# A decode block on Trainium2: the first weight load in two pieces, and exps that write the probability block themselves

## The chip, the cores and the metric

The kernel runs on one core of one Trainium2 chip. The metric is the device time of one execution, in microseconds. A core has five engines that run side by side, each with its own instruction queue: TensorE (PE, matmuls; PEld is its weight load), VectorE (DVE), ScalarE (ACT), GpSimd (POOL) and SyncE (SP), which here only issues transfers. Sixteen DMA engines move the data between device memory (HBM) and the core's memory of 128 partitions (SBUF). Engines wait for each other through semaphores.

## What is computed

One token passes through a transformer block: layer norm, attention over a cache of 4096 positions with 32 heads of 128, a residual, a second layer norm, a gated feed-forward part, a residual. All inputs are bf16.

```python
q = (layernorm(x) @ wq).reshape(B, Sq, Hq, Dh).transpose(0, 2, 1, 3)
scores = einsum("bhqd,bhkd->bhqk", q, k) * (Dh ** -0.5)
p = softmax(scores)
o = einsum("bhqk,bhkd->bhqd", p, v)
h = x + o.reshape(B, Sq, Hq * Dh) @ wo
h2 = h + (gelu(layernorm(h) @ w_gate) * (layernorm(h) @ w_up)) @ w_down
```

With a single token every weight and every cache entry is used once: 84 MB are read from HBM. The caches alone are 2 x 32 heads x 4096 x 128 x 2 bytes = 67 MB.

## The kernel before

**How the work is laid out.** The 32 heads are cut into eight groups of four. In a group, partition 32j + p holds head j's positions 128p to 128p + 127, so a group's K or V is a tile of 128 partitions of 32,768 bytes each (4 MB). Three slots hold such tiles in turn (`NSLOT`, L22). The order of loads is K0, V0, K1, K2, V1, K3, V2 and so on to K7, V6, V7 (L173 to L176): K runs one group ahead of V.

**The loads.** All large loads are issued by SP, in program order, on one queue. First comes wq (L172), 5 MB into `arena`, 128 partitions of 40,960 bytes. `issue` (L186) then issues cache loads as slots come free: load n waits for `consumed[n - 3]`, the last reader of the tile that lay in its slot. For a K tile that reader is the last product of the group on DVE, for a V tile the last matmul of `pv_group`. While SP waits for one slot, every later load waits behind it. The output projection's weights follow into `arena` (L387), and then the feed-forward weights into the slots. `emit({"sync": 2})` (L474) places SP's first two issues, wq and K0, ahead of the start barrier that all engines pass; SP's others come after it.

**The start.** `x_row` is loaded from ACT's queue; the layer norm runs on PE, DVE and ACT; `q_proj` (L260) waits for it and for wq, and leaves q in `qb`, one head's q repeated over its 32 partitions.

**A stage.** A group has four stages of 32 positions per partition. In stage s, `score_mult` (L274) multiplies K by q on DVE into `prod` (128x4096) and PE folds the 128 products of each position to 16 by eight matmuls with an identity matrix, into one of two PSUM banks. `score_exp` (L291) then sums the 16 on DVE into `sc` (L293). The program has stage s + 1's product ahead of stage s's sum on DVE.

**The end of a group.** After the fourth stage ACT takes one exp over the group's whole 128x128 scores into `pt` (L297) and adds up each partition's exps into a column of `RS`. DVE then multiplies `pt` by `own` (`block_diag`, L300): `own[p, j]` is 1 where partition p belongs to head j, otherwise 0. The result `p_bd` (128 x 128 x 4) holds, for each position, four columns, of which a partition fills only its own head's. `pv_group` (L306) uses it as the weights of 32 matmuls with V as the moving operand, on PE after the next group's folds; ACT copies the sums to SBUF (L319), and four small matmuls add them up (`head_sum`, L321). `own` comes from a select on POOL (L225) and a reduction on DVE (L233).

**Each half of the heads.** `sum_half` (L332) multiplies `RS` by `own`, sums it over the partitions by a matmul and takes the reciprocal; `finish_half` (L339) scales. Then come the output projection (L350), the second layer norm, the gated part and the down projection.

`P.op` records every instruction with the events that it waits for; `emit` writes them out engine by engine in the order of the program, so SP's issues all stand at L51 in the profile.

Of the kernel before, what the change touches and what calls it, by code (L numbers as in the profile page):

```python
# [5 lines left out]
FP32 = mybir.dt.float32  # L6
BF16 = mybir.dt.bfloat16
ALU = mybir.AluOpType
ACTF = mybir.ActivationFunctionType
AX = mybir.AxisListType  # L10

D = 640
H = 32
# [4 lines left out]
INV_SQRT_DH = 1.0 / math.sqrt(DH)  # L18
GELU_C0 = math.sqrt(2.0 / math.pi)
GELU_C1 = 0.044715  # L20
NG = 8
# [80 lines left out]
def bass_sequential_preLN__gqa_block_cached__glu_gated_geglu__decode_kernel(nc, A_x, A_k_cache, A_v_cache, A_wq, A_wo, B_x, B_w_gate, B_w_up, B_w_down, out):  # L102
    sb = lambda name, shape, dt: nc.alloc_sbuf_tensor(name, shape, dt)
    SLOT = 10 * DF
    slots = [sb("slot%d" % i, [128, SLOT], BF16) for i in range(NSLOT)]
    arena = sb("arena", [128, 5 * 4096], BF16)
    prod = sb("prod", [128, 4, 32, DH], BF16)
    qb = sb("qb", [128, NG, DH], BF16)
    sc = sb("sc", [128, 2, 128], FP32)
    pt = sb("pt", [128, 2, 128], BF16)  # L110
    own_t = sb("own_t", [128, 4, 32], BF16)
    own = sb("own", [128, 4], BF16)
    p_bd = sb("p_bd", [128, 2, 128, 4], BF16)
    RS = sb("RS", [128, NG], FP32)
    RT = sb("RT", [128, NG, 4], FP32)
    x_row = sb("x_row", [1, D], BF16)
    out_row = sb("out_row", [1, D], BF16)
    xx = sb("xx", [128, 10], FP32)
# [23 lines left out]
    ones_f = sb("ones_f", [128, 128], FP32)  # L142
    mean_f = sb("mean_f", [128, 128], FP32)
    ones_b = sb("ones_b", [128, 1024], BF16)
# [3 lines left out]
    zero_t = sb("zero_t", [128, 1], FP32)  # L148
    bank = [nc.alloc_psum_tensor("bank%d" % i, [128, 512], FP32) for i in range(8)]
    ps_f = [bank[0], bank[1]]  # L150
# [6 lines left out]
    ps_z = bank[6]  # L157
# [5 lines left out]
    P = Prog(nc)  # L163
    V = lambda fn, *d: P.op("vector", fn, *d)
    A = lambda fn, *d: P.op("scalar", fn, *d)
    T = lambda fn, *d: P.op("tensor", fn, *d)
    GP = lambda fn, *d: P.op("gpsimd", fn, *d)
# [1 line left out]

    A(lambda e: e.preload_act_table_set("natural_log_exp_and_others"))  # L170
    d_x = P.dma("scalar", x_row[:, :], A_x[0, :, :])
    d_wq = [P.dma("sync", arena[:, :], A_wq[:, :].rearrange("(p c) n -> p (c n)", c=5))]  # L172
    order = [("K", 0), ("V", 0), ("K", 1)]  # L173
    for G in range(1, NG - 1):
        order += [("K", G + 1), ("V", G)]
# [2 lines left out]
    landed, consumed = {}, {}  # L178
# [7 lines left out]
    def issue(upto):  # L186
        while state["next"] < min(upto, len(order)):
# [8 lines left out]
                         for i in range(parts)]  # L196
# [9 lines left out]
    c_eps = V(lambda e: e.memset(zero_t[:, :], 0.0))  # L206
    c_onesb = GP(lambda e: e.memset(ones_b[:, :], 1.0))
    c_idb = GP(lambda e: e.affine_select(id_b[:, :], ones_b[:, 0:128], pattern=[[1, 128]], compare_op=ALU.is_equal,
                                         fill=0.0, base=0, channel_multiplier=-1), c_onesb)
    c_idf = GP(lambda e: e.affine_select(id_f[:, :], ones_f[:, :], pattern=[[1, 128]], compare_op=ALU.is_equal,  # L210
                                         fill=0.0, base=0, channel_multiplier=-1), c_ones)
    c_sel = GP(lambda e: e.affine_select(sel[:, :, :], ones_b[0:16, :].rearrange("p (a b) -> p a b", a=8),
                                         pattern=[[-1, 8], [1, 128]], compare_op=ALU.is_equal,
                                         fill=0.0, base=0, channel_multiplier=-8), c_onesb)
    GP(lambda e: e.memset(hs[:, :, :], 0.0))
    c_hs = GP(lambda e: e.affine_select(hs_t[:, :, :], ones_f[:, 0:64].rearrange("p (a b) -> p a b", a=4),
                                        pattern=[[-32, 4], [-1, 16]], compare_op=ALU.is_equal,
                                        fill=0.0, base=0, channel_multiplier=1), c_ones)
    c_sel2 = GP(lambda e: e.affine_select(sel2[:, :, :], ones_b[0:64, 0:128].rearrange("p (a b) -> p a b", a=64),
                                          pattern=[[1, 64], [0, 2]], compare_op=ALU.is_equal,  # L220
                                          fill=0.0, base=0, channel_multiplier=-1), c_onesb)
    c_par = GP(lambda e: e.affine_select(par_t[:, :, :], ones_b[:, 0:128].rearrange("p (a b) -> p a b", a=2),
                                         pattern=[[-1, 2], [-2, 64]], compare_op=ALU.is_equal,
                                         fill=0.0, base=0, channel_multiplier=1), c_onesb)
    c_own = GP(lambda e: e.affine_select(own_t[:, :, :], ones_b[:, 0:128].rearrange("p (a b) -> p a b", a=4),  # L225
                                         pattern=[[-32, 4], [-1, 32]], compare_op=ALU.is_equal,
                                         fill=0.0, base=0, channel_multiplier=1), c_onesb)

    c_po = [V(lambda e, b=b: e.memset(bank[b][:, :], 0.0)) for b in (2, 4)]
    c_hs = V(lambda e: e.reduce_sum(hs[:, :, 12:16], hs_t[:, :, :].rearrange("p t (g j) -> p g j t", g=4), axis=AX.X), c_hs)  # L230

    V(lambda e: e.reduce_sum(par[:, :], par_t[:, :, :], axis=AX.X), c_par)
    V(lambda e: e.tensor_reduce(own[:, :], own_t[:, :, :], axis=AX.X, op=ALU.max), c_own)  # L233


    def x_cols(e):
# [32 lines left out]
    qc = A(lambda e: e.copy(qb[:, 4:8, :].rearrange("p g d -> p (g d)"), ps_q[1][:, :]), qd)  # L269


    folds, reds, exps, blocks, pvs, evs, hds = {}, {}, {}, {}, {}, {}, {}

    def score_mult(s):  # L274
        G, n = s // 4, pos[("K", s // 4)]
        kt = view(n)
        u = s % 4
        m = V(lambda e: e.tensor_tensor(  # L278
            out=prod[:, s % 4, :, :], in0=kt[:, 32 * u:32 * u + 32, :],
            in1=qb[:, G, :].unsqueeze(1).to_broadcast([128, 32, DH]), op=ALU.mult),  # L280
            landed[n][0], qa, qc, folds.get(s - 4))
        consumed[n] = m

        def fold(e):
            for b in range(8):
                i = e.matmul(ps_f[s % 2][:, :], id_b[:, :], prod[:, s % 4, :, 16 * b:16 * b + 16],  # L286
                             start=(b == 0), stop=(b == 7))
            return i
        folds[s] = T(fold, m, c_idb, reds.get(s - 2))

    def score_exp(s):  # L291
        G = s // 4
        reds[s] = V(lambda e: e.reduce_sum(  # L293
            sc[:, G % 2, 32 * (s % 4):32 * (s % 4) + 32], ps_f[s % 2][:, :].rearrange("p (g d) -> p g d", d=16), axis=AX.X),
            folds[s], exps.get(G - 2))
        if s % 4 == 3:
            exps[G] = A(lambda e: e.activation(pt[:, G % 2, :], sc[:, G % 2, :], ACTF.Exp, bias=zero_t[:, 0:1],  # L297
                                               scale=INV_SQRT_DH, accum_out=RS[:, G:G + 1]), reds[s], blocks.get(G - 2), c_eps)

    def block_diag(G):  # L300
        blocks[G] = V(lambda e: e.tensor_tensor(  # L301
            out=p_bd[:, G % 2, :, :], in0=pt[:, G % 2, :].unsqueeze(2).to_broadcast([128, 128, 4]),
            in1=own[:, :].unsqueeze(1).to_broadcast([128, 128, 4]), op=ALU.mult), exps[G], pvs.get(G - 2))


    def pv_group(G):  # L306
        n = pos[("V", G)]
        vt = view(n)
        po = ps_o[G % 2]
        parts = len(landed[n])  # L310
        for k in range(parts):
            def pv(e, k=k):
                for b in range(32 // parts * k, 32 // parts * (k + 1)):
                    a = 32 * (b % 4)
                    i = e.matmul(po[a:a + 16, :], p_bd[:, G % 2, 4 * b:4 * b + 4, :].rearrange("p g j -> p (g j)"),  # L315
                                 vt[:, 4 * b:4 * b + 4, :], start=(b < 4), stop=(b >= 28))
                return i
            pvs[G] = consumed[n] = T(pv, blocks[G], landed[n][k], evs.get(G - 2), *c_po)
        evs[G] = A(lambda e: e.copy(po_sb[:, G % 2, :], po[:, :]), pvs[G], hds.get(G - 2))  # L319

        def head_sum(e):  # L321
            g = G % 4
            for r in range(4):
                i = e.matmul(ps_a[0:16, 128 * (G // 4):128 * (G // 4) + 128], hs[:, r, 12 - 4 * g:28 - 4 * g],  # L324
                             po_sb[:, G % 2, 128 * r:128 * r + 128], start=(g == 0 and r == 0), stop=(g == 3 and r == 3))
            return i
        return head_sum
# [2 lines left out]
    zs = {}  # L330

    def sum_half(t):  # L332
        gs = slice(4 * t, 4 * t + 4)
        r = V(lambda e: e.tensor_tensor(out=RT[:, gs, :], in0=RS[:, gs].unsqueeze(2).to_broadcast([128, 4, 4]),  # L334
                                        in1=own[:, :].unsqueeze(1).to_broadcast([128, 4, 4]), op=ALU.mult), exps[4 * t + 3])
        z = T(lambda e: e.matmul(ps_z[0:16, 0:1], RT[:, gs, :].rearrange("p g j -> p (g j)"), ones_f[:, 0:1], start=True, stop=True), r)  # L336
        zs[t] = V(lambda e: e.reciprocal(rz[:, t:t + 1], ps_z[0:16, 0:1]), z)

    def finish_half(t):  # L339
# [20 lines left out]
    def scores(G):  # L360
        for i in range(4):
            score_mult(4 * G + i)
            if i >= 1:
                score_exp(4 * G + i - 1)
        score_exp(4 * G + 3)
        block_diag(G)
        issue(pos[("K", G)] + 1 + NSLOT)

    heads = None
    for kind, G in order:  # L370
        if kind == "K":
            scores(G)
            continue
        if G in (3, NG - 1):
            sum_half(G // 4)
        if heads is not None:
            hds[G - 1] = T(heads, evs[G - 1], c_hs, qa, qc)
        if G == 4:
            a0 = finish_half(0)
        heads = pv_group(G)  # L380
        issue(pos[("V", G)] + 1 + NSLOT)
# [22 lines left out]
             for a, lo, hi in ((0, 0, 4), (1, 0, 4), (2, 0, 3), (2, 3, 4))]  # L404
# [10 lines left out]
                                     in1=hT[:, 0:5].unsqueeze(1).to_broadcast([128, 128, 5]), op=ALU.mult), h, c_idf)  # L415
# [33 lines left out]
    def down(ms, qs=range(4)):  # L449
        def fn(e):  # L450
            for m in ms:
                for q in qs:
# [6 lines left out]
                              start=True, stop=True), g9, c_sel2)  # L459
# [11 lines left out]
    d_out = P.dma("sync", out[0, :, :], out_row[:, :], *os)  # L471
    P.op("sync", None, d_out)

    P.emit({"sync": 2})  # L474


# [26 lines left out]
```

## Time and profile before

| | us |
|---|---|
| median of three runs (lowest, highest) | 205.05 (204.47, 205.85) |
| the profiled execution: its time | 205.85 |
| its span, first to last instruction | 204.5 |
| busy: PE, DVE, ACT, POOL | 119.8, 106.5, 12.6, 4.3 |
| products on DVE, L278, 32 of them | 72.4 (2.28 each) |
| sums on DVE, L293, 32 | 22.0 (0.69 each) |
| mask multiplies on DVE, L301, 8 | 5.5 (0.69 each) |
| exps on ACT, L297, 8 | 3.2 (0.40 each) |
| wq from its issue to its landing | 15.9 |

The profile covers one execution. A group of instructions is a line of the kernel, an engine, an operation and a tile, with the number of instructions, their busy time and the mean of one; behind it stands how long the engine was idle before them and what ended that. "Chain" is the work that ended last, followed back from the last instruction to whatever released each step. The slices cut the span into 40 equal parts; a digit is a busy share in tenths, with 9 for 90% and more. In tables by stretch, the last two numbers are the DMA share and GB/s, and the one before them is the clock that TensorE was granted. A DMA packet is one contiguous run that one DMA engine moves.

### The profile page before, as it was taken

The numbers are of one execution on the slowest core, as the hardware profiler recorded it, in microseconds if no ns is written. First come the engines' busy times: TensorE is split into PE (matmuls) and PEld (weight loads), VectorE is DVE, ScalarE is ACT, GpSimd is POOL, SyncE is SP. The second block draws the span as 40 slices with busy tenths as digits, with TensorE's granted clock in tenths as the row PEclk, the third lists the DMA queues.
The fourth block names the chain that finished last, engine by engine and source line by source line (L and its number), as shares of the span: only waits on it lengthen the run. The fifth ranks groups of instructions, "written<-read, shape, count | busy, mean of one in ns | idle before, by whom it ended". The sixth has DMA issues, their size and how long they took to land.

```text
span 204.5 us, 2243 instructions
## 1 busy us (share of the span) xinstructions
PE 119.8 (59%) x1010; PEld 58.7 (29%) x1010; DVE 106.5 (52%) x115; ACT 12.6 (6%) x33; POOL 4.3 (2%) x13
## 2 busy tenths in 40 slices
PE   0108058447837786670694585729662988467495
PEld 0103023112212252240231332303231335266383
DVE  3300188627967969921795379357827772100221
ACT  2100100010000001020000100010020002100101
POOL 7000000000000000000000000000000000000000
PEclk9999999965896999996589969996996699955555
DMA  9999999999999989999999999999999999999991
GB/s 353 409 438 436 410 410 474 436 420 410 449 449 430 410 301 415 410 436 462 429 417 410 471 429 429 410 436 455 429 420 410 423 430 428 428 416 422 409 394 51
DMA packets 4333, 84.37 MB, mean 413 GB/s; under 512 B 482, under 2 KB 868, under 8 KB 1508
## 3 DMA queue, kind: packets, MB, share of 16 engines
q1 hardware_dynamic: 4322, 84.23, 96.8%
q8 instruction: 8, 0.13, 0.3%
q14 instruction: 1, 0.01, 0.0%
q10 hardware_dynamic: 2, 0.00, 0.0%
HBM read 84.23 MB, written 0.00 MB: 412 GB/s over the span
## 4 chain that ended last, share of the span: by engine, by line
DMA 63%; DVE 17%; PE 16%; SPq 2%; issue 1%; ACT 0%
DMA slot<-in_A_k_cache_dram 41%; DVE prod L278 13%; DMA slot<-in_A_v_cache_dram 11%; DMA slot<-in_B_w_down_dram 11%; PE bank L286 11%; PE bank L315 3%; DVE sc L293 3%; SPq L51 2%; PE bank L324 1%; DVE p_bd L301 1%; ACT pt L297 0%; PE bank L454 0%; DVE out_row L467 0%; PE bank L336 0%; DVE RT L334 0%
## 5 line engine op out<-in xcount | busy, mean ns | idle before, releaser
L286 PE MATMUL bank<-prod,id_b 128*128 128x512 bf16 x256 | 73.9, 447 | 52.0 <-DVE prod L278 52.0
L278 DVE TENSOR_TENSOR prod<-slot,qb 128x4096 bf16<-128x4096 bf16 x32 | 72.4, 2283 | 25.4 <-DMA slot<-in_A_k_cache_dram 25.4
L286 PEld LDWEIGHTS bank<-prod,id_b 128*128 128x128 bf16 x256 | 26.6, 112 | 100.2 <-DVE prod L278 65.2
L293 DVE TENSOR_REDUCE sc<-bank 128x32 f32<-128x512 f32 x32 | 22.0, 686 | 20.8 <-PE bank L286 20.8
L315 PE MATMUL bank<-slot,p_bd 128*16 128x512 bf16 x256 | 17.8, 389 | 2.6 <-DVE p_bd L301 2.0
L315 PEld LDWEIGHTS bank<-slot,p_bd 128*16 128x16 bf16 x256 | 9.5, 90 | 6.9 <-DVE p_bd L301 2.5
L297 ACT ACTIVATE pt<-sc,zero_t 128x128 bf16<-128x128 f32 x8 | 3.2, 402 | 126.3 <-DVE sc L293 126.3
L324 PE MATMUL bank<-po_sb,hs 128*16 128x128 f32 x64 | 8.4, 274 | 1.4 <-ACT po_sb L319 1.4
L264 PE MATMUL bank<-arena,xlnB 128*32 128x512 bf16 x40 | 4.5, 629 | 7.8 <-DMA arena<-in_A_wq_dram 7.8
L354 PE MATMUL bank<-aP,arena 128*128 128x1 bf16 x160 | 6.7, 178 | 3.8 <-DMA arena<-in_A_wo_dram 3.8
L424 PE MATMUL bank<-hlnT,slot 128*128 128x1 bf16 (+1 forms) x140 | 6.7, 176 | 3.0 <-DMA slot<-in_B_w_gate_dram 3.0
L301 DVE TENSOR_TENSOR p_bd<-pt,own 128x512 bf16<-128x512 bf16 x8 | 5.5, 692 | 4.5 <-ACT pt L297 4.5
L354 PEld LDWEIGHTS bank<-aP,arena 128*128 128x128 bf16 x160 | 6.6, 131 | 3.9 <-DMA arena<-in_A_wo_dram 2.6
L424 PEld LDWEIGHTS bank<-hlnT,slot 128*128 128x128 bf16 (+1 forms) x140 | 6.3, 118 | 3.9 <-DVE hX L414 3.1
L324 PEld LDWEIGHTS bank<-po_sb,hs 128*16 128x16 f32 x64 | 5.6, 96 | 4.7 <-issue 2.1
L268 DVE CAST qb<-bank 128x512 bf16<-128x512 f32 x1 | 0.7, 691 | 10.7 <-PE bank L264 10.7
L319 ACT COPY po_sb<-bank 128x512 f32<-128x512 f32 x8 | 4.7, 586 | 19.9 <-PE bank L315 18.4
L411 DVE TENSOR_TENSOR hT<-xx,bank 128x5 f32<-128x5 f32 x1 | 0.2, 161 | 10.2 <-PE bank L354 10.2
L264 PEld LDWEIGHTS bank<-arena,xlnB 128*32 128x32 bf16 x40 | 1.6, 140 | 9.8 <-issue 9.8
L238 PE MATMUL bank<-one_bf,x_row 1*128 1x1 bf16 x5 | 0.4, 177 | 6.8 <-DMA x_row<-in_A_x_dram 6.8
L340 DVE TENSOR_SCALAR aT<-bank,rz 16x128 bf16<-16x128 f32 x2 | 0.7, 336 | 5.8 <-PE bank L324 5.8
L439 DVE COPY g_t<-bank 128x14 f32<-128x14 f32 x1 | 0.2, 172 | 4.2 <-PE bank L424 4.2
(66 smaller groups left out, 27.7 us busy)
## 6 DMA issues: line engine op xcount, KB each, us to landing
slot<-in_A_k_cache_dram SPq DMA_DIRECT2D x8, 4096.0 KB, 20.6
slot<-in_A_v_cache_dram SPq DMA_DIRECT2D x7, 4096.0 KB, 17.8
arena<-in_A_wq_dram SPq DMA_DIRECT2D x1, 5120.0 KB, 15.9
slot<-in_A_v_cache_dram SPq DMA_DIRECT2D x2, 2048.0 KB, 20.2
arena<-in_A_wo_dram SPq DMA_DIRECT2D x1, 2560.0 KB, 27.6
slot<-in_B_w_gate_dram SPq DMA_DIRECT2D x1, 2160.0 KB, 15.2
arena<-in_A_wo_dram SPq DMA_DIRECT2D x1, 1920.0 KB, 31.7
slot<-in_B_w_up_dram SPq DMA_DIRECT2D x1, 1296.0 KB, 17.8
```

What stands on the lines that cost most here:

```text
L51: ev = self.op(eng, lambda e: e.dma_start(out, in_), *deps, dma=True)
L264: i = e.matmul(ps_q[hf][32 * j:32 * j + 32, :], xlnB[:, c, :], wq_j[:, c, j, 4 * hf:4 * hf + 4, :], start=(c == 0), stop=(c == 4))
L278: m = V(lambda e: e.tensor_tensor(out=prod[:, s % 4, :, :], in0=kt[:, 32 * u:32 * u + 32, :], in1=qb[:, G, :].unsqueeze(1).to_broadcast([1 ...
L286: i = e.matmul(ps_f[s % 2][:, :], id_b[:, :], prod[:, s % 4, :, 16 * b:16 * b + 16], start=(b == 0), stop=(b == 7))
L293: reds[s] = V(lambda e: e.reduce_sum(sc[:, G % 2, 32 * (s % 4):32 * (s % 4) + 32], ps_f[s % 2][:, :].rearrange("p (g d) -> p g d", d=16), ...
L297: exps[G] = A(lambda e: e.activation(pt[:, G % 2, :], sc[:, G % 2, :], ACTF.Exp, bias=zero_t[:, 0:1], scale=INV_SQRT_DH, accum_out=RS[:, G ...
L301: blocks[G] = V(lambda e: e.tensor_tensor(out=p_bd[:, G % 2, :, :], in0=pt[:, G % 2, :].unsqueeze(2).to_broadcast([128, 128, 4]), in1=own[ ...
L315: i = e.matmul(po[a:a + 16, :], p_bd[:, G % 2, 4 * b:4 * b + 4, :].rearrange("p g j -> p (g j)"), vt[:, 4 * b:4 * b + 4, :], start=(b < 4) ...
L319: evs[G] = A(lambda e: e.copy(po_sb[:, G % 2, :], po[:, :]), pvs[G], hds.get(G - 2))
L324: i = e.matmul(ps_a[0:16, 128 * (G // 4):128 * (G // 4) + 128], hs[:, r, 12 - 4 * g:28 - 4 * g], po_sb[:, G % 2, 128 * r:128 * r + 128], s ...
L354: r = e.matmul(ps_p[:, c:c + 1], wo_sb[:, t, i, c::5], aP[:, t, i:i + 1], start=(t == 0 and c == 0 and i == 0), stop=(t == 1 and i == 15), ...
L424: i = e.matmul(ps[0:128 if m < 13 else 64, m:m + 1], ws, hlnT[:, c:c + 1], start=(c == 0 and m == 0), stop=(c == 4), skip_group_check=True)
```

## The change

Two things change together.

1. The wq load becomes two loads on the same queue: partitions 0 to 15, then partitions 16 to 127. `q_proj` waits for both. SP's early issues become three: both pieces and K0.
2. There is no exp per group, no `pt`, no `own` and no multiply. Instead `p_bd` and `RS` are set to zero once on POOL, and after each stage's sum ACT takes four exps, one per head: head j's 32 partitions by the stage's 32 positions, written straight into column j of `p_bd` (every fourth element), with the sum of the exps added to an own element of `RS`. `sc` has one buffer for each of four stages. `sum_half` sums the four stages' parts in place of the multiply.

```diff
-    sc = sb("sc", [128, 2, 128], FP32)
-    pt = sb("pt", [128, 2, 128], BF16)
-    own_t = sb("own_t", [128, 4, 32], BF16)
-    own = sb("own", [128, 4], BF16)
+    sc = sb("sc", [128, 4, 32], FP32)
...
-    RS = sb("RS", [128, NG], FP32)
-    RT = sb("RT", [128, NG, 4], FP32)
+    RS = sb("RS", [128, H, 4], FP32)
+    RT = sb("RT", [128, H], FP32)
...
-    d_wq = [P.dma("sync", arena[:, :], A_wq[:, :].rearrange("(p c) n -> p (c n)", c=5))]
+    wq_v = A_wq[:, :].rearrange("(p c) n -> p (c n)", c=5)
+    d_wq = [P.dma("sync", arena[lo:hi, :], wq_v[lo:hi, :]) for lo, hi in ((0, 16), (16, 128))]
...
-    c_own = GP(lambda e: e.affine_select(own_t[:, :, :], ...
+    c_pbd = GP(lambda e: e.memset(p_bd[:, :, :, :], 0.0))
+    c_rs = GP(lambda e: e.memset(RS[:, :, :], 0.0))
...
-    V(lambda e: e.tensor_reduce(own[:, :], own_t[:, :, :], axis=AX.X, op=ALU.max), c_own)
...
-            sc[:, G % 2, 32 * (s % 4):32 * (s % 4) + 32], ps_f[s % 2][:, :].rearrange("p (g d) -> p g d", d=16), axis=AX.X),
-            folds[s], exps.get(G - 2))
-        if s % 4 == 3:
-            exps[G] = A(lambda e: e.activation(pt[:, G % 2, :], sc[:, G % 2, :], ACTF.Exp, bias=zero_t[:, 0:1],
-                                               scale=INV_SQRT_DH, accum_out=RS[:, G:G + 1]), reds[s], blocks.get(G - 2), c_eps)
-
-    def block_diag(G):
-        blocks[G] = V(lambda e: e.tensor_tensor(
-            out=p_bd[:, G % 2, :, :], in0=pt[:, G % 2, :].unsqueeze(2).to_broadcast([128, 128, 4]),
-            in1=own[:, :].unsqueeze(1).to_broadcast([128, 128, 4]), op=ALU.mult), exps[G], pvs.get(G - 2))
+            sc[:, s % 4, :], ps_f[s % 2][:, :].rearrange("p (g d) -> p g d", d=16), axis=AX.X),
+            folds[s], exps.get(s - 4))
+        for j in range(4):
+            x = A(lambda e, j=j: e.activation(
+                p_bd[32 * j:32 * j + 32, G % 2, 32 * (s % 4):32 * (s % 4) + 32, j],
+                sc[32 * j:32 * j + 32, s % 4, :], ACTF.Exp,
+                bias=zero_t[32 * j:32 * j + 32, 0:1], scale=INV_SQRT_DH,
+                accum_out=RS[32 * j:32 * j + 32, 4 * G + j, s % 4:s % 4 + 1]),
+                reds[s], pvs.get(G - 2), c_pbd, c_rs, c_eps)
+        exps[s] = x
...
-            pvs[G] = consumed[n] = T(pv, blocks[G], landed[n][k], evs.get(G - 2), *c_po)
+            pvs[G] = consumed[n] = T(pv, exps[4 * G + 3], landed[n][k], evs.get(G - 2), *c_po)
...
-        gs = slice(4 * t, 4 * t + 4)
-        r = V(lambda e: e.tensor_tensor(out=RT[:, gs, :], in0=RS[:, gs].unsqueeze(2).to_broadcast([128, 4, 4]),
-                                        in1=own[:, :].unsqueeze(1).to_broadcast([128, 4, 4]), op=ALU.mult), exps[4 * t + 3])
+        hh = slice(16 * t, 16 * t + 16)
+        r = V(lambda e: e.reduce_sum(RT[:, hh], RS[:, hh, :], axis=AX.X), exps[16 * t + 15])
...
-        block_diag(G)
...
-    P.emit({"sync": 2})
+    P.emit({"sync": 3})
```

More of the change, by code (lines that the diff above doesn't have):

```diff
@@ L224, in bass_sequential_preLN__gqa_block_cached__glu_gated_geglu__decode_kernel @@
                                          fill=0.0, base=0, channel_multiplier=1), c_onesb)
-    c_own = GP(lambda e: e.affine_select(own_t[:, :, :], ones_b[:, 0:128].rearrange("p (a b) -> p a b", a=4),
-                                         pattern=[[-32, 4], [-1, 32]], compare_op=ALU.is_equal,
-                                         fill=0.0, base=0, channel_multiplier=1), c_onesb)
+    c_pbd = GP(lambda e: e.memset(p_bd[:, :, :, :], 0.0))
+    c_rs = GP(lambda e: e.memset(RS[:, :, :], 0.0))
     c_po = [V(lambda e, b=b: e.memset(bank[b][:, :], 0.0)) for b in (2, 4)]
@@ L269, in bass_sequential_preLN__gqa_block_cached__glu_gated_geglu__decode_kernel @@
     qc = A(lambda e: e.copy(qb[:, 4:8, :].rearrange("p g d -> p (g d)"), ps_q[1][:, :]), qd)
-    folds, reds, exps, blocks, pvs, evs, hds = {}, {}, {}, {}, {}, {}, {}
+    folds, reds, exps, pvs, evs, hds = {}, {}, {}, {}, {}, {}
     def score_mult(s):
@@ L332, in sum_half @@
     def sum_half(t):
-        gs = slice(4 * t, 4 * t + 4)
-        r = V(lambda e: e.tensor_tensor(out=RT[:, gs, :], in0=RS[:, gs].unsqueeze(2).to_broadcast([128, 4, 4]),
-                                        in1=own[:, :].unsqueeze(1).to_broadcast([128, 4, 4]), op=ALU.mult), exps[4 * t + 3])
-        z = T(lambda e: e.matmul(ps_z[0:16, 0:1], RT[:, gs, :].rearrange("p g j -> p (g j)"), ones_f[:, 0:1], start=True, stop=True), r)
+        hh = slice(16 * t, 16 * t + 16)
+        r = V(lambda e: e.reduce_sum(RT[:, hh], RS[:, hh, :], axis=AX.X), exps[16 * t + 15])
+        z = T(lambda e: e.matmul(ps_z[0:16, 0:1], RT[:, hh], ones_f[:, 0:1], start=True, stop=True), r)
         zs[t] = V(lambda e: e.reciprocal(rz[:, t:t + 1], ps_z[0:16, 0:1]), z)
```

## The prediction

> **What bounds the kernel now.** I read the page from the top: busy shares, slices, queues, then the chain of work that ended last, then the stretches around the one hole in the transfers.
>
> ```profile
> PE 119.8 (59%) x1010; PEld 58.7 (29%) x1010; DVE 106.5 (52%) x115; ACT 12.6 (6%) x33; POOL 4.3 (2%) x13
> DMA  9999999999999989999999999999999999999991
> q1 hardware_dynamic: 4322, 84.23, 96.8%
> HBM read 84.23 MB, written 0.00 MB: 412 GB/s over the span
> ```
>
> No compute engine passes 59%, while the queue that SP feeds keeps the sixteen DMA engines at work 96.8% of the time. The bound is the stream of loads. A compute instruction matters only where it delays the release of a slot so long that the stream runs dry, and a load matters by what it costs the stream. The row of DMA tenths has one 8 inside, slice 15. The chain shows what led there:
>
> ```profile
> 44.98 0.02 issue
> 45.00 2.30 DVE prod L278
> ...
> 59.39 0.50 ACT pt L297 x2
> 59.90 0.02 issue
> 59.92 0.69 DVE p_bd L301
> 60.61 2.21 DVE prod L278
> ...
> 69.95 2.21 DVE prod L278
> ```
>
> K of group 1 lands at 44.98. From there to 72.16 the chain runs on DVE and PE through groups 1 and 2, and in its middle stand one exp (0.50) and one mask multiply (0.69), between two groups' products. At 72.17 SP issues V of group 2 into the slot just freed. The DMA share (1.00 is all sixteen engines) in one-microsecond stretches:
>
> ```profile
> 70.00:71.00 1.00, 1.00 (x7) 0.39 (x4) 1.00 (x1) 0.00 (x0) 0.00 (x0) 1.00 0.91 393
> 71.00:72.00 1.00, 0.30 (x2) 0.00 (x0) 1.00 (x1) 0.00 (x0) 0.00 (x0) 1.00 0.46 197
> 72.00:73.00 1.00, 0.80 (x4) 0.41 (x5) 0.74 (x2) 0.00 (x0) 0.00 (x0) 1.00 0.16 66
> 73.00:74.00 1.00, 1.00 (x6) 0.29 (x3) 0.00 (x0) 0.00 (x0) 0.00 (x0) 1.00 1.67 459
> ```
>
> A packet is counted where it starts, so single shares swing; what counts is the 0.16 after 72. The trace's packet records say it exactly: fourteen engines finish K of group 3 between 71.93 and 72.37, the last two at 73.66 and 74.00; the first packet of V starts at 73.13, 0.96 after its issue. The loads' last landings are 9.68 us apart before and after, but 12.42 apart across the hole (74.00 to 86.42). **The hole costs the last engine 2.74 us**, and the last engine sets the end.
>
> **The change, first part: exps and mask.** Per group it removes one exp of 128x128 (0.40, and 0.19 for reading its accumulator; 0.50 together) and one multiply (0.69). DVE idles 0.56 ahead of each multiply (4.5 us over 8). Eight of these leave DVE: 8 x (0.69 + 0.56) = 10 us, of which only the one in the chain above is on a path that ends in a hole: 0.69 + 0.56 = 1.25. The other slot releases come 4 to 12 us before the stream would run dry (V of group 3: issued 86.11, queue full until 93.15), so their shares are worth nothing; the transfers in flight cover them.
>
> It adds 128 exps of 32x32, each with an accumulator read, where there were 8. The nearest rows bound one: 0.29 us (a 128x1 activation at L249) to 0.40 + 0.19. Four per stage are 1.2 to 2.4 us; a stage lasts 2.28 + 0.60 = 2.88 us on DVE, so ACT keeps up even at the upper end. Reduce s waits for exp s-4, three stages back: cover 8 us. Behind the exps on ACT stands the copy of L319, after the next group's exps as before; it needs pv's end, 1.5 us after the last exp was done at 75.4, so at most 1 us of it shows, and its reader is next group's head sum, 10 us off. pv of group 0 waits for four exps, not exp and multiply (1.27 together): 0 to 1.1 later, before V of group 1 is issued at 43.70, whose queue is full until 52.5: hidden. The exps' wait on pv of group G-2 is met, since those matmuls are ahead of group G's folds on PE. POOL loses a select (0.30) and gains two memsets (0.95 and some 0.2, from ones_b and ones_f), DVE loses own's reduce (0.28); all end by 7 us, and the first exp comes at 32. sum_half's reduce replaces a 0.10 multiply by about 0.26 (row L230) under a running load.
>
> So V of group 2 is issued at 72.17 - 1.25 = 70.92, its packets can start at 71.88, just when the first engines run out (71.93). Bounds of the gain: 0 if the shift brings nothing, 1.25 if it only shifts, 2.74 if the hole closes. I take the middle of the last two, **-2.0**.
>
> **Second part: the split load.** One issue of wq (0.38) becomes two. K of group 0 is issued some 0.4 us later, and the barrier behind SP's early issues (the others start at 1.25) moves as much; both lie under a load that lasts until 15.5, and the layer norm, ready at 9.8, has 6 us to spare. The bytes stay: 128 packets of 40,960 B, eight for each engine. In the trace, 112 of them take 1.51 us and the sixteen first ones, all started together, 2.06 to 2.64, median 2.23. What a packet takes when sixteen rows lie on neighbouring partitions, or 112 rows are dealt out seven to an engine, no row shows; every large load here covers 128 partitions. Lower bound: packets queue with no gap between loads (a semaphore packet takes 0.01), so 0; a gain is excluded, as an engine with 1.51 per packet has nothing faster beside it in this size. Upper bound: seven further packets per engine as slow as the slowest, 7 x (2.64 - 1.51) = 7.9. At the median first packet it is 7 x (2.23 - 1.51) = 5.0. The nearest rows are these first packets, sixteen engines at once in rows of the same load, and since a load lands with its slowest engine I take the middle of 5.0 and 7.9: **+6.4**. Nothing hides it: the queue is full from the start and every later load is behind it.
>
> [...]
>
> **The sum.** +6.4 - 2.0 = +4.4. The profiled execution took 205.85 (span 204.5 and 1.35 around it), the slowest of three, and becomes 210.25; on the median of 205.05 it is **209.5**, which I forecast. Own range: 0.72 for one slow first packet more, less 1.25, is no loss, so the case starts where the packets are slow throughout: 5.0 - 2.74 = +2.3 to 7.9 - 1.25 = +6.6, or 207.3 to 211.7.
>
> **Rivals.**
>
> 1. *The split is free and the hole closes (faster).* Place: V of group 2 at 72. Packets of both pieces run at 1.51; the gain is 1.25 to 2.74: 202.3 to 203.8. For it: packets follow one another without a gap across loads everywhere else. Against: every one of those loads has 128 partitions. It decides once a wq packet costs less than 2.0/7 = 0.29 us above 1.51.
> 2. *Near cancellation.* Only the second piece's first packet is slow (+0.72 to +1.13), and the hole gives 1.25 or the exps eat some of that: 204.5 to 206.2. For it: slow packets appear only where engines start from empty (again at 73.1, 1.73 to 2.50 for 1.21). [...]
> 3. *The stream pays far more.* The number of engines that a load uses follows its rows: x_row, one row, is one packet on one engine. Were 112 rows carried by eight engines, fourteen each, wq would last 14 x 1.51 + 1.51 = 22.7 in place of 12.1: +10.6 - 2.0, 213.7. For it: only that row. Against: 112 is seven times sixteen.
> 4. *Removing the multiply does nothing*, because the last engine's hole has another cause than the late issue (it alone starts 1.0 to 1.3 after the others at the span's start too). The forecast then becomes 211.5; it lies in the forecast's own range.
>
> **Chances and range.** Forecast (with rival 4) 0.53, rival 1 0.22, rival 2 0.15, rival 3 0.10. About 1% is what a measurement of this kernel can tell from no change, 203.0 to 207.1. Faster by more: two thirds of rival 1, 0.15. Within: the rest of it, rival 2 and a sliver of the forecast, 0.25. Slower: 0.60. The range reaches down through rival 1 and up to rival 3's figure: 202.5 to 214.0.
>
> **What would show it.** The arena packets: their duration after the first, and when the load lands (16.0 now; 21 to 24 if I am right, 16 if rival 1 is, 26 or more if rival 3 is). The first product's start at 25.57 moves by as much. DVE goes from the last reduce of a group to the next product with no exp between. V of group 2 is issued 25.9 us after K of group 1 landed (27.2 now), and slice 15's 8 is gone. ACT's busy time rises from 12.6 to between 48 and 83, still with a reduce waiting for no exp. The prediction is wrong in its main step if the wq packets still take 1.51, and in its second if the landings across group 2's V stay 12 us apart.

## The result and the profile after

| | before | after |
|---|---|---|
| median (lowest to highest), us | 205.04 (204.29 to 205.85), 6 runs | 215.63 (215.3 to 216.02), 6 runs |
| profiled execution: time, span | 205.85, 204.5 | 215.3, 214.1 |

The changed kernel is slower: ratio 1.0516, 95% interval 1.0484 to 1.0549, some 10.6 us. The forecast was slower, but 209.5, and 215.6 lies above its range. Slower was right; the size was not, and nearly all of the miss lies in the wq load: alone it cost 12.6 where 6.4 had been counted, while the exps' part gave 1.3 where 2.0 had been.

The page of the changed kernel, the same lines as before:

```profile
PE 119.6 (56%) x1010; PEld 58.3 (27%) x1010; DVE 101.1 (47%) x106; ACT 61.1 (29%) x273; POOL 5.0 (2%) x14
DMA  9989899999999999999999999999999999999993
GB/s 122 245 245 245 214 435 441 416 465 392 462 416 418 459 404 447 419 423 455 410 453 416 423 444 416 455 410 435 441 410 450 416 410 432 430 415 426 408 415 129
q1 hardware_dynamic: 4338, 84.23, 97.9%
HBM read 84.23 MB, written 0.00 MB: 394 GB/s over the span
```

The same row of the kernel before:

```profile
GB/s 353 409 438 436 410 410 474 436 420 410 449 449 430 410 301 415 410 436 462 429 417 410 471 429 429 410 436 455 429 420 410 423 430 428 428 416 422 409 394 51
```

This is the trap of the case. By the DMA tenths the sixteen engines are nearly as busy as ever (two 8s at the start), and slice 15's 8 is gone. But the row of GB/s says that in the first five slices (5.35 us each) they moved 122 to 245 GB/s, and 392 to 465 from then on, the last slice aside; before, the first five have 353 to 438. The share counts the time that packets are under way, and the wq packets behind the first sixteen took 2.82 us (median) where they had taken 1.51. The time is lost in the first 27 us, with busy engines. The changed kernel's wait for wq on PE, and the first matmul behind it:

```profile
PE bank L260 <- DMA arena<-in_A_wq_dram: 11.3, 1, 11.3
```

```profile
15.16 0.35 PE L234 MATMUL bank<-one_bf,x_row 1*128 1x1 bf16 x5 [15.16 <-DMA x_row<-in_A_x_dram]
17.71 0.44 DVE L249 TENSOR_SCALAR xlnB<-xx,ln 128x160 bf16<-128x160 f32 x1 [0.69 <-ACT ln L246]
27.82 2.75 PE L260 MATMUL bank<-arena,xlnB 128*32 128x512 bf16 x24 [11.26 <-DMA arena<-in_A_wq_dram]
```

Before:

```profile
16.00 4.46 PE L264 MATMUL bank<-arena,xlnB 128*32 128x512 bf16 x40 [7.79 <-DMA arena<-in_A_wq_dram]
```

The first matmul on wq starts at 27.82 in place of 16.00. The layer norm is late as well (x_row came at 15.2 in place of 6.8; its packet started at 12.21 in place of 4.86, between those of wq), yet 10 us ahead of wq.

The packet records give the last landing, over the sixteen engines, of each load: wq 26.78 (15.50 before), K of group 1 56.27 (44.54), K of group 3 85.85 (74.00), V of group 2 95.85 (86.42). So the stream is 11.3 us late after wq, 11.9 after K of group 3, and 9.4 after V of group 2: the hole gave some 2.4 back there. The stretch of the changed kernel in which the hole would lie shows no share near the 0.16 of before:

```profile
82.00:83.00 1.00, 1.00 (x23) 0.88 (x25) 0.28 (x1) 0.67 (x4) 0.00 (x0) 1.00 0.68 295
83.00:84.00 1.00, 1.00 (x21) 0.56 (x13) 0.00 (x0) 0.97 (x6) 0.00 (x0) 1.00 0.91 393
84.00:85.00 1.00, 0.25 (x2) 0.00 (x0) 0.00 (x0) 0.58 (x1) 0.00 (x0) 1.00 1.15 492
```

Two theories of the 11.3 us were to be told apart: that a load's packets are slow because of the partitions that it writes (destination), or because of something else in the split, be it a second beginning, an odd number of rows, or the rows read at once (source).

### The profile page after: what moved, and what is told of

The parts are those of the page before. It is cut to its first block, busy times and chain, and to the rows that moved or that the text cites. A ratio compares the mean times of both kernels' runs of the same rounds, so it can differ in the third digit from the quotient of the medians.

```text
span 214.1 us, 2506 instructions
## 1 busy us (share of the span) xinstructions
PE 119.6 (56%) x1010; PEld 58.3 (27%) x1010; DVE 101.1 (47%) x106; ACT 61.1 (29%) x273; POOL 5.0 (2%) x14
## 4 chain that ended last, share of the span: by engine, by line
DMA 58%; DVE 19%; PE 14%; issue 4%; another core or an unknown queue 2%; SPq 2%
DMA slot<-in_A_k_cache_dram 37%; DVE prod L274 15%; DMA slot<-in_B_w_down_dram 10%; DMA slot<-in_A_v_cache_dram 10%; PE bank L282 9%; DVE sc L289 3%; PE bank L311 3%; SPq L51 2%; PE bank L320 1%; PE bank L448 0%; DVE out_row L461 0%; PE bank L331 0%; DVE RT L330 0%
## 5 line engine op out<-in xcount | busy, mean ns | idle before, releaser
L282 PE MATMUL bank<-prod,id_b 128*128 128x512 bf16 x256 | 72.5, 440 | 51.5 <-DVE prod L274 51.5
L293 ACT ACTIVATE p_bd<-sc,zero_t 32x32 bf16<-32x32 f32 x128 | 46.4, 362 | 84.1 <-DVE sc L289 82.9
L282 PEld LDWEIGHTS bank<-prod,id_b 128*128 128x128 bf16 x256 | 26.0, 110 | 98.8 <-DVE prod L274 65.1
L293 ACT ACTIVATION_READ_ACCUMULATOR p_bd<-sc,zero_t 32x1 f32 x128 | 23.5, 184 | 0.0
L311 PE MATMUL bank<-slot,p_bd 128*16 128x512 bf16 x256 | 18.8, 409 | 3.3 <-ACT p_bd L293 2.5
L260 PE MATMUL bank<-arena,xlnB 128*32 128x512 bf16 x40 | 4.5, 631 | 11.3 <-DMA arena<-in_A_wq_dram 11.3
L234 PE MATMUL bank<-one_bf,x_row 1*128 1x1 bf16 x5 | 0.4, 177 | 15.2 <-DMA x_row<-in_A_x_dram 15.2
L245 ACT ACTIVATE ln<-ln,eps_t 128x1 f32<-128x1 f32 x2 | 0.6, 294 | 28.1 <-DVE ln L243 28.1
L315 ACT COPY po_sb<-bank 128x512 f32<-128x512 f32 x8 | 4.7, 585 | 11.3 <-PE bank L311 11.3
L265 ACT CAST qb<-bank 128x512 bf16<-128x512 f32 x1 | 0.6, 585 | 14.7 <-PE bank L260 14.7
## 6 DMA issues: line engine op xcount, KB each, us to landing
slot<-in_B_w_gate_dram SPq DMA_DIRECT2D x1, 2160.0 KB, 15.2
```

Of the source, the lines that this page charges most:

```text
L260: i = e.matmul(ps_q[hf][32 * j:32 * j + 32, :], xlnB[:, c, :], wq_j[:, c, j, 4 * hf:4 * hf + 4, :], start=(c == 0), stop=(c == 4))
L293: x = A(lambda e, j=j: e.activation(p_bd[32 * j:32 * j + 32, G % 2, 32 * (s % 4):32 * (s % 4) + 32, j], sc[32 * j:32 * j + 32, s % 4, :], ...
```

## The experiments

Ten kernels ran. The first four take the change apart.

**The exps' part alone**: the changed kernel with wq whole.

```diff
-    d_wq = [P.dma("sync", arena[lo:hi, :], wq_v[lo:hi, :]) for lo, hi in ((0, 16), (16, 128))]
+    d_wq = [P.dma("sync", arena[:, :], wq_v)]
...
-    P.emit({"sync": 3})
+    P.emit({"sync": 2})
```

> The changed kernel with wq in one load again: the exps' part of the change alone. Theory (the exps' part closes the hole at V of group 2, the split alone costs the time): landings across that load 9.7 us apart in place of 12.4, wq landed near 16, time 2.0 to 2.7 below before, 202.3 to 203. Rival (the exps cost time on ACT or through their waits, and the loss is shared between the two parts): 205 or more.

Measured: 203.28 against 204.58 before, ratio 0.9942 (0.9902 to 0.9983): 1.3 us faster, clear of the noise but less than the 2.0 to 2.7 that were expected. The trace of this kernel where the hole was:

```profile
71.00:72.00 1.00, 1.00 (x8) 0.42 (x6) 0.25 (x1) 0.98 (x6) 0.00 (x0) 1.00 0.95 393
72.00:73.00 1.00, 1.00 (x22) 0.89 (x23) 0.44 (x1) 0.58 (x5) 0.00 (x0) 1.00 0.93 393
73.00:74.00 1.00, 1.00 (x24) 0.70 (x14) 0.00 (x0) 0.98 (x6) 0.00 (x0) 1.00 1.22 492
```

The 0.16 after 72 has become 0.93. The last landings of K of group 3 and V of group 2 are 10.29 apart (12.42 before, 9.7 between most other loads), so some 0.6 remains.

**The split alone**: the kernel before with the changed kernel's two loads and `emit({"sync": 3})`.

> The kernel before with only the split of wq. Theory (the split costs about 11.7 us at the start and the hole at V of group 2 stays): wq landed near 27, time 205.0 + 11.7 = 216.7, or up to 2 less if the uneven engines happen to cover the hole. Rival (part of the loss belongs to the exps): 208 to 213.

Measured: 217.16, ratio 1.0614 (1.0582 to 1.0646), 12.6 us slower; wq landed at 26.95, and the hole stayed (76.12 to 85.83 for K of group 3, then 97.69: 11.86). So the split costs more than the whole change, and the exps' part gives some back. The two parts add up to 12.6 - 1.3 = 11.3, the change measured 10.6; the difference is of the size by which repeated runs of one kernel differ.

**The same split, by columns**: two loads, 1/8 and 7/8 of the bytes, each over all 128 partitions.

```diff
+    d_wq = [P.dma("sync", arena[:, lo:hi], wq_v[:, lo:hi]) for lo, hi in ((0, 2560), (2560, 20480))]
```

> The changed kernel, wq split the other way: both pieces cover all 128 partitions, the first 1/8 of the columns, the second 7/8; the same two issues, the same bytes in each. Theory (the cost is which partitions a piece covers): wq packets of both pieces at their size over 27 KB per us, time as with one load, 202.3 to 203.2. Rival (the cost is that there are two loads at the start, a second slow beginning): 209 to 216.

Measured: 203.22, ratio 0.994 (0.9915 to 0.9965); wq landed at 14.37. Two loads, the same bytes in each, the same issues: no cost. A second beginning is not it.

**The mask multiply kept, but later**: the kernel before; only the order on DVE differs.

```diff
+    late = []
+
+    def flush():
+        while late:
+            block_diag(late.pop(0))
...
             score_mult(4 * G + i)
+            if i == 0:
+                flush()
...
-        block_diag(G)
+        late.append(G)
...
+        if G in late:
+            flush()
         heads = pv_group(G)
```

> The kernel before, its mask multiply of a group emitted on DVE after the next group's first product (for group 0 and 7, right ahead of their V matmuls). No work is removed; only the multiply and the wait for the exp leave the path to the release of K2's slot. Theory (the hole is the late issue of V of group 2): issue about 1.2 us earlier against K1's landing, hole gone, 202.3 to 203.2. Rival (the hole has another cause, and e1's gain, if any, is from less work on DVE): 204.5 to 205.5.

Measured: 203.21, ratio 0.9943 (0.9914 to 0.9973), the exps' gain without any work removed. The first product of group 1 in this kernel, and SP's issue of V of group 2:

```profile
44.30 4.49 DVE L278 TENSOR_TENSOR prod<-slot,qb 128x4096 bf16<-128x4096 bf16 x2 [3.83 <-DMA slot<-in_A_k_cache_dram]
```

```profile
69.75 0.33 SPq L51 DMA_DIRECT2D slot<-in_A_v_cache_dram  x1
```

That is 25.45 us after the product began; before it was 27.17 (45.00 to 72.17):

```profile
72.17 0.33 SPq L51 DMA_DIRECT2D slot<-in_A_v_cache_dram  x1
```

The same two rows of the changed kernel:

```profile
56.82 4.49 DVE L274 TENSOR_TENSOR prod<-slot,qb 128x4096 bf16<-128x4096 bf16 x2 [5.04 <-DMA slot<-in_A_k_cache_dram]
```

```profile
79.62 0.33 SPq L51 DMA_DIRECT2D slot<-in_A_v_cache_dram  x1
```

| kernel | V of group 2 issued after group 1's first product began, us | landings of K of group 3 and V of group 2 apart, us |
|---|---|---|
| before | 27.17 | 12.42 |
| split alone | 27.06 | 11.86 |
| exps alone | 25.51 | 10.29 |
| multiply later | 25.45 | 10.29 |
| changed | 22.80 | 10.00 |

The hole is the late issue, and in this kernel what closes most of it is where the multiply stands, not that there is one. The changed kernel's 22.80 has a second cause, which the prediction did not count: the clock that TensorE was granted. Before, the first folds of group 1 and of group 2 ran at 0.50 of full speed (rows of the trace: 42.5 to 52.7 us, 63.0 to 66.4), in the changed kernel at 1.00 (57.1 to 87.8). The first eight folds of group 1 take 3.61 us before (the first half of the sixteen below) and 1.90 in the changed kernel:

```profile
47.35 6.26 PE L286 MATMUL bank<-prod,id_b 128*128 128x512 bf16 x16 [3.69 <-DVE prod L278]
```

```profile
59.17 1.90 PE L282 MATMUL bank<-prod,id_b 128*128 128x512 bf16 x8 [2.14 <-DVE prod L274]
```

So DVE's first sum began 5.98 and 5.93 us after the first product of its group (groups 1 and 2) before, and 4.41 and 4.40 in the changed kernel. That is 3.1 of the 4.4 by which the issue came earlier; the exp and the multiply are the rest. What moved the stretches of full clock was not tested.

The next four change only how wq is cut, on the changed kernel.

**Two halves**, partitions 0 to 63 and 64 to 127:

```diff
-    ... for lo, hi in ((0, 16), (16, 128))]
+    ... for lo, hi in ((0, 64), (64, 128))]
```

> The changed kernel with wq cut into partitions 0 to 63 and 64 to 127. [...] Rival A (an odd row count, 112, or one row for each engine is what is slow): packets at 1.5, 202.5 to 204. [...]

**Eight loads of sixteen neighbours:**

```diff
+    d_wq = [P.dma("sync", arena[16 * i:16 * i + 16, :], wq_v[16 * i:16 * i + 16, :]) for i in range(8)]
...
+    P.emit({"sync": 9})
```

> The changed kernel with wq in eight loads of 16 neighbouring partitions, all ahead of K0. Theory (destination): each piece reaches the same few paths, packets near 6 us each (the first piece's were 4.3 to 5.5), wq about 8 x 6 = 48 us, time 202.6 + 36 = 239. Rival A (a piece's beginning costs something once): 202.6 + 8 x 0.7 to 1.1 = 208 to 211. Rival B (source: neighbouring rows of memory read at once are slow): 239 too; the next two kernels tell B from the theory.

**Eight loads of sixteen partitions that lie eight apart:**

```diff
+    d_wq = [P.dma("sync", arena[i::8, :], wq_v[i::8, :]) for i in range(8)]
```

> Wq in eight loads of 16 partitions that lie 8 apart (i, i+8, ... i+120), sources likewise. [...] Rival A: as eight neighbouring pieces, 208 to 211. Rival B (source): anything from 203 to 215, told by the next.

**Destination as in the second, source as in the third:**

```diff
+    d_wq = [P.dma("sync", arena[16 * i:16 * i + 16, :], wq_v[i::8, :]) for i in range(8)]
```

> Wq in eight loads of 16 neighbouring partitions as destination, but each reads every eighth row of wq: the rows of wq reach other partitions, so q is built from mixed-up rows; work and sizes are unchanged. Theory (destination decides): as the eight neighbouring pieces, about 239. Rival B (source decides): as the strided one, about 215 or below.

Measured, with the median duration of a wq packet of 40,960 B after the first sixteen:

| wq is cut into | packet, us | last landing of wq | time | ratio (95%) |
|---|---|---|---|---|
| one load (before) | 1.51 | 15.50 | 204.29 in this round | |
| two halves | 3.20 | 27.25 | 216.44 | 1.0585 (1.0538 to 1.0632) |
| eight of 16 neighbours | 5.80 | 47.71 | 236.85 | 1.1583 (1.1522 to 1.1644) |
| eight of 16, eight apart | 3.18 | 27.71 | 216.97 | 1.0611 (1.0563 to 1.0659) |
| neighbours, source eight apart | 5.72 | 47.57 | 236.78 | 1.158 (1.1528 to 1.1632) |

Source rows that lie eight apart change next to nothing (5.72 for 5.80); with the same source rows, destination partitions that lie eight apart nearly halve the packets (3.18 for 5.72). For these loads the destination decides. Two even halves are slow too, so an odd number of rows is not it. The rate shows in the windows; first the eight loads of neighbours, then those with the other source (last column GB/s):

```profile
5.00:45.00 40.00, 0.95 (x7) 0.77 (x7) 3.05 (x14) 1.85 (x3) 4.80 (x10) 1.00 1.02 115
```

```profile
5.00:45.00 40.00, 0.95 (x7) 0.77 (x7) 2.93 (x13) 1.67 (x3) 4.63 (x10) 1.00 1.01 115
```

A DMA share of 1.0 and 115 GB/s, where the kernel before moves 437 in its first load:

```profile
5.00:8.00 3.00, 0.74 (x7) 0.66 (x7) 0.88 (x4) 0.00 (x0) 0.37 (x2) 1.00 1.01 437
8.00:11.00 3.00, 0.21 (x1) 0.11 (x1) 0.82 (x3) 0.59 (x2) 0.00 (x0) 1.00 1.01 437
```

Sixteen packets of 40,960 B in 5.80 us are 113 GB/s, in 3.20 us 205, and in the 1.51 us of the one load 434. Why packets to neighbouring partitions take longer was not shown.

What stayed unexplained was the larger piece: it covers 112 of the 128 partitions, and still its packets took 2.2 to 3.4 us (medians of its seven steps in the changed kernel). Two kernels ask how these rows are given to the engines.

**The pieces the other way round**, `((0, 112), (112, 128))`:

> The changed kernel with the pieces the other way round: partitions 0 to 111 first, then 112 to 127. It tells how much of the loss belongs to which piece. Theory (each piece costs by the partitions that it reaches, wherever it stands): the 112 rows at 2.1 to 3.0 us a packet, seven in some 18 us, the 16 rows in about 5.8, wq landed near 26, time as changed, 215 to 216.5. Rival (the second piece was slow only because it followed the first and met its late packets): the 112 rows at 1.5 to 1.9, wq landed near 20, 209 to 210.

**The 112 rows as seven loads of sixteen partitions, seven apart:**

```diff
+    d_wq = [P.dma("sync", arena[i:112:7, :], wq_v[i:112:7, :]) for i in range(7)]
+    d_wq += [P.dma("sync", arena[112:128, :], wq_v[112:128, :])]
...
+    P.emit({"sync": 9})
```

> Partitions 0 to 111 as seven loads of 16 partitions that lie seven apart (i, i+7, ... i+105), then 112 to 127 in one. [...]

Measured: 214.95, ratio 1.0495 (1.0447 to 1.0544), and 215.23, ratio 1.0509 (1.0461 to 1.0557), with wq landed at 25.81 and 26.12: the order of the pieces makes little difference, and the seven loads cost what the one of 112 costs. Even the steps agree. The packet records, sixteen packets at a time in order of start, shortest/median/longest in us:

```
112 first:   2.13/2.69/3.45  2.72/2.88/2.99  2.68/2.70/2.96  1.73/2.08/2.81  1.80/1.83/2.64  2.49/2.72/2.90  2.60/2.65/2.96  4.02/4.89/5.35
seven apart: 1.75/2.50/3.32  2.85/2.87/2.95  2.80/2.84/2.97  1.86/2.22/2.89  1.84/1.86/2.70  2.41/2.74/2.89  2.69/2.78/3.00  3.83/4.66/5.08
```

The last column is the load of 112 to 127; the seven before it are the 112 rows. If the load of 112 rows gives each engine seven neighbouring rows, its sixteen engines write partitions seven apart at every step, as the seven loads do, and the like steps fit that; but the packet records name no partition, so it is inferred. Steps 4 and 5 are the quick ones (medians 1.8 to 2.2; the other five 2.5 to 2.9). In the changed kernel, where the 112 rows begin at partition 16, they are steps 3 and 4 (2.16 and 2.38; the other steps 2.66 to 3.35). No packet of these rows is as quick as the 1.51 of the one load: the shortest takes 1.73, and with 112 first the shortest packet is 2.4 or more in four of the seven steps. Why all sixteen engines are held, and two steps less than the others, was not settled. Nor was the source varied by itself for these rows: the seven loads read them seven rows apart, and the load of 112 does too if it is dealt as inferred.

By the same inference a load of 128 rows is not dealt in runs of eight: that would be the loads of sixteen, eight apart, at 3.18, and its packets take 1.51.

## Why the prediction was wrong

- **The bound** was read rightly: the stream of loads. What wq lost, 11.3 us, is still there at K of group 3 (11.9), and nothing hid it.
- **The split, +6.4: the step that failed.** It measured 26.78 - 15.50 = 11.3 at wq's landing and 12.6 alone. The prediction took for its upper bound seven packets at the slowest first packet, 2.64, and called these the nearest rows. They were not of the kind: a start from empty, against packets that are slow by the partitions that they write together. Packets took up to 5.5 in the 16-row piece and had a median of 2.8 in the other. Taken apart with the packets' medians: the first piece 4.98 for 2.23, +2.8, which the prediction's sum had put at nothing; and the seven steps behind it 19.0 for 7 x 1.51 = 10.6, +8.5, where the sum had 5.0 to 7.9. So both terms were too small. The larger loss is in the 112 rows.
- **Rival 3** had nearly the right loss at wq (+10.6) with a wrong mechanism: all sixteen engines carried the 112 rows, seven each (seven steps of sixteen packets). That was luck, and by the prediction's own sign (wq landing at 26 or more; it landed at 26.8) it would have been taken for confirmed. Only the packets' durations tell the two apart.
- **Rival 1**, the free split, fell with the split alone; that packets follow each other without a gap says nothing about where they write. **Rival 2** fell with the same records: every step of wq was slow (medians 2.16 to 4.98), not only a first packet.
- **The exps, -2.0.** Direction and mechanism were right, the size was too large; the kernel with the multiply later shows the cause. Between landings 2.1 came back in the run with the exps alone and 2.4 in the changed kernel, but by the medians only 1.3: the profiled execution of before was its slowest run and its hole of 2.74 probably longer than in most. That last is argued, not shown; the one other trace with the hole, the split alone, has 11.86 - 9.71 = 2.15. The issue came 1.66 earlier against K1's product in the kernel with the exps alone (44.27 to 69.78) where 1.25 was counted: 1.24 is the exp and the multiply, as counted, and 0.42 is from DVE's first sums, which began 5.88 and 5.61 us after the first product of groups 1 and 2 in place of 5.98 and 5.93. That these folds ran in part at a higher clock is the author's estimate, from the changed kernel. In the changed kernel the issue came 22.80 after the product, not 25.9 after the landing as the prediction's sign said, and most of that (3.1 of 4.4) is the clock. So the hole there would have closed for two reasons, and the prediction had one of them.
- **Rival 4**, another cause of the hole, fell with the exps alone and with the kernel that only moves the multiply.
- **ACT** went to 61.1, within the 48 to 83 given (its own rows make the lower bound 45). One exp takes 0.36 and its accumulator 0.18, and they follow one another every 0.43, 1.7 us for four; the 2.88 of a stage cover them, and no reduce waits for an exp:

```profile
DVE sc L289 <- PE bank L282: 19.9, 14, 1.5
```

The wait of pv of group 0 lies within its bounds: it starts 2.49 us after PE was free, 2.04 before, so 0.45 later where 0 to 1.1 was given, and it stays hidden.

## What to carry to other kernels

If a load like this one has to be cut, cut it along its columns, not along its partitions: pieces of the same bytes cost nothing one way (203.22 against 203.28 with one load) and 12.6 us the other (217.16 against 204.58). Read the DMA share together with GB/s, since engines that are held in slow packets count as busy: 1.02 at 115 GB/s with packets of 5.80 us. And an instruction worth removing from a busy engine may be worth as much when it only moves behind the one that releases a transfer: 203.2 to 203.3 either way here, the best of all versions.

## What was not expected of the hardware

- Of the 112 rows, written with sixteen packets at a time, every step is slow on all sixteen engines: a median of 2.8 us a packet in the changed kernel for 1.51 in the load of 128 rows. Sixteen partitions seven apart in each of seven loads show the same steps; eight apart they take 3.18.
- In the kernel before, the hole cost more than its width: the stream ran dry for some 1.0 us on most engines, the last one got its first packet at 75.45, 3.3 us after the issue, and that packet took 2.50 in place of 1.21 (the other first packets 1.38 to 2.44); the landings were 2.74 late.
- Issuing the first load took SP 0.39 us for 16 or 112 neighbouring partitions, 0.55 for 64 neighbours and 0.58 for 16 that lie eight apart. The issue of K of group 0, the same in all of these, took 0.42 to 0.43 behind the former and 0.59 behind the latter, so the load ahead counts too.
